# The first layer of both mixtures for the second half of the tokens by Strassen's 2x2 blocks (7 products for 8), with joined float32 weights kept in DRAM and read back

## Chip, cores and metric

The kernel runs on one core of one Trainium2 chip. The metric is device time in microseconds for one execution, here the median of the runs. In the texts "TensorE" is PE of the profile (PEld its weight loads), "VectorE" DVE, "ScalarE" ACT, "GpSimd" POOL, and SP is the queue that issues most DMAs.

## What is computed

An attention with two mixings of the heads (b = 4, 12 heads, 448 tokens of 64), then two layers on all 1792 tokens x 768:

```
h = (x @ w1) * (x @ w2) @ w3          # w1, w2: 768 x 1024, w3: 1024 x 1024
x = h @ w_out                         # w_out: 1024 x 768
h = maximum(x @ w_in, 0)              # w_in: 768 x 2048
return h * h @ w_out2                 # w_out2: 2048 x 768
```

All in float32; the kernel multiplies w3 by w_out once on the chip and uses the product.

## The kernel before

Attention takes the first third or so of the time; the change leaves it as it is. What follows is class `Moe`. The tokens lie in two halves `hf` of 896, each of two blocks `t` of 448 columns (`TB`). Feature chunks of 128 lie on the partitions.

A float32 product is made of three matmuls (`mm3`, L54): each operand is split into a high and a low part, w x = wh xh + wh xl + wl xh. A matmul has a 128x128 piece of weights and 448 columns of tokens.

The work of a half is a list of units. `l1` (16 units: eight output chunks `m`, for w1 and for w2) has 6 input chunks x 3 = 18 matmuls for each `t`; w1's result is copied to SBUF by ScalarE (L645), w2's is multiplied with it on VectorE (L649), and the product is split into `bhab` (ScalarE, L623) and `blab` (VectorE, L624). `ly` (6 units of 2 x 24 matmuls) multiplies by the joint w3 w_out. `l3` (16 units of 2 x 18, in two groups of 8) is the first layer of the second mixture: relu on ScalarE (L695), square on VectorE (L697), split into `bhh` and `blh`. `l4` (6 units of 2 x 24 after each group of l3) is its second layer.

Weights arrive as 64-bit words: `raw` by a DMA on SP (L69), `y` by a ScalarE copy (`narrow`, L81), three VectorE operations that put the float32 bits together (`join`, L93, L95, L97) into `f`. ScalarE then makes the high part `wh` (`high`, L111) and GpSimd the low part `wl` (`rest`, L115; VectorE for the pieces of w_out). There are 4 buffers of `raw`, 2 of `y`, 2 of `f`, 8 each of `wh` and `wl`. `stage(s)` sets the order on every engine: load piece s+6, narrow s+4, join s+3, low part of s+2, the unit's matmuls, high part of s+3. Each half brings all its weights through this chain anew; the first half also mixes the making of w3 w_out (`p34`) into l1.

## Time and profile before

| | |
|---|---|
| runs | 1362.34 us median (1362.15, 1362.34, 1362.64) |
| span of the profiled execution | 1361.7 us, that is 0.6 less than the median |
| its mean granted TensorE clock | 0.992 of full speed |
| first half: l1 with p34, ly, l3 and l4 | about 480 to 955 us |
| second half: l1 | 955 to 1070 us |
| second half: ly | 1070 to 1128 us |
| second half: l3, l4, l3, l4 | 1128 to 1362 us, some 57 us each |

The profile gives for each engine the time that it was busy. A stage's bound is read from the stage: which engine is busy without a break there, and what the others wait for. "Busy" counts an instruction from its start to its end, a stretch in which it waits for a port included.

### The profile page before, as it was taken

The page shows a single profiled execution, that of the slowest core. Times are in us where ns is not written, and L with a number is a line of the kernel's source. Part 1 is how long each engine was busy: PE and PEld are TensorE (multiplying, and loading weights), DVE is VectorE, ACT ScalarE, POOL GpSimd, SP SyncE. Part 2 cuts the span into 40 slices and gives each one's busy share as a digit, 9 for nine tenths or more (in the row PEclk, how much of TensorE's full clock was granted, in tenths as well). Part 3 has the DMA queues.
Part 4 walks back from the last instruction along what each step waited for, and adds up shares of the span by engine and source line. Part 5 has one row for each costly group of instructions (what it writes and reads, how often), then busy time and mean ns, then how long its engine had stood idle before and what let it go on. Part 6 is the DMA issues. An engine that isn't in the chain of part 4 may idle for free.

```text
span 1361.7 us, 23959 instructions
## 1 busy us (share of the span) xinstructions
PE 1318.2 (97%) x8858; PEld 1145.5 (84%) x8858; DVE 925.8 (68%) x1586; ACT 707.0 (52%) x1525; POOL 377.3 (28%) x399
## 2 busy tenths in 40 slices
PE   4999999999998799999999999999999999999998
PEld 2677777776776678899999999999999999999998
DVE  3798788788787689964218954985555228945972
ACT  4877878787886455534224533543343224533530
...
GB/s 145 189 176 189 123 198 198 138 168 203 144 122 170 119 164 168 189 181 131 60 66 109 128 119 79 121 185 181 120 117 95 62 78 101 133 120 80 124 149 57
DMA packets 97033, 183.76 MB, mean 135 GB/s; under 512 B 20693, under 2 KB 63701, under 8 KB 96469
## 3 DMA queue, kind: packets, MB, share of 16 engines
...
HBM read 129.52 MB, written 14.16 MB: 106 GB/s over the span
## 4 chain that ended last, share of the span: by engine, by line
PE 81%; issue 6%; ACT 4%; DVE 3%; POOL 3%; DMA 2%; SPq 0%; ACTq 0%; POOLq 0%; DVEq 0%
PE l L54 46%; PE y L54 8%; PE sp L281 7%; PE tp L337 5%; PE p L54 5%; PE pv L378 5%; PE sc L255 4%; ACT p L295 1%; POOL wl L115 1%; DMA r<-s 1%; POOL ql L238 1%; ACT ph L320 1%; ACT s L266 1%; DMA kraw<-k 1%; DVE pl L327 1%
## 5 line engine op out<-in xcount | busy, mean ns | idle before, releaser
L115 POOL TENSOR_TENSOR wl<-f,wh 128x384 fp32r<-128x384 f32 (+1 forms) x176 | 197.9, 1127 | 568.8 <-ACT wh L111 542.0
L93 DVE TENSOR_SCALAR f<-y 128x384 int32<-128x384 int32 (+1 forms) x208 | 149.3, 718 | 93.2 <-POOL wl L115 89.8
L281 PE MATMUL sp<-r,kpre 120*120 120x448 f32 x360 | 159.2, 564 | 6.2 <-DMA r<-s 3.5
L111 ACT ACTIVATE wh<-f 128x384 fp32r<-128x384 f32 (+1 forms) x192 | 106.7, 556 | 104.4 <-DVE f L97 96.1
L295 ACT ACTIVATE p<-sp,nm 120x448 f32<-120x448 f32 x180 | 113.7, 639 | 69.7 <-DVE nm L287 69.1
L54 PE MATMUL l<-bhh,wh 128*128 128x448 f32 x384 | 139.4, 363 | 0.0
L54 PE MATMUL l<-bhh,wl 128*128 128x448 f32 x384 | 139.2, 362 | 0.0
L54 PE MATMUL l<-blh,wh 128*128 128x448 f32 x384 | 138.2, 360 | 0.0
L287 DVE TENSOR_REDUCE nm<-sp 120x1 f32<-120x448 f32 x180 | 108.2, 620 | 41.5 <-PE sp L281 35.3
L97 DVE SCALAR_TENSOR_TENSOR f<-raw,f 128x384 int32<-128x384 int32 (+1 forms) x208 | 130.9, 629 | 7.2
L95 DVE SCALAR_TENSOR_TENSOR f<-y,f 128x384 int32<-128x384 int32 (+1 forms) x208 | 128.9, 620 | 7.0
L337 PEld LDWEIGHTS <-ph 120*128 120x128 f16 (+1 forms) x1440 | 108.0, 99 | 29.4 <-issue 28.9
L337 PE MATMUL tp<-kwh,ph 120*128 120x120 f16 x720 | 121.5, 219 | 3.8 <-DVE p L352 2.3
L327 DVE SCALAR_TENSOR_TENSOR pl<-p,sm,ph 120x448 f16<-120x448 f32 x180 | 124.5, 733 | 0.0
L337 PE MATMUL tp<-kwh,pl 120*128 120x120 f16 x720 | 120.7, 218 | 1.1 <-DVE pl L327 1.1
L81 ACT ACTIVATE y<-raw 128x384 f32<-128x384 f32 (+1 forms) x208 | 120.1, 577 | 1.5 <-DMA raw<-w3t 1.5
L337 PE MATMUL tp<-kwl,ph 120*128 120x120 f16 x720 | 120.7, 218 | 0.0
L320 ACT ACTIVATE ph<-p,sm 120x448 f16<-120x448 f32 x180 | 112.0, 683 | 16.0 <-DVE sm L315 15.8
L255 PE MATMUL sc<-kt,qh 128*110 128x448 f32 (+1 forms) x192 | 101.1, 527 | 16.2 <-DVE kt L216 14.6
L310 POOL TENSOR_SCALAR sm<-sm 120x2 f32<-120x2 f32 (+3 forms) x94 | 30.9, 329 | 273.0 <-ACT p L295 261.3
L281 PEld LDWEIGHTS sp<-r,kpre 120*120 120x120 f32 x360 | 58.9, 184 | 48.3 <-issue 21.4
L266 ACT ACTIVATE s<-sc 110x448 f32<-110x448 f32 (+1 forms) x186 | 90.5, 554 | 15.9 <-PE sc L255 15.9
(112 smaller groups left out, 3109.6 us busy)
## 6 DMA issues: line engine op xcount, KB each, us to landing
r<-s SPq DMA_DIRECT2D x172, 210.0 KB
...
```

The source lines that it names most:

```text
L54: nc.tensor.matmul(acc, w, x, start=(first and i == 0 and j == 0), stop=(last and i == n - 1 and j == 2))
L81: nc.scalar.activation(y, self.raw[i][:, :, 1].bitcast(F), AF.Copy, scale=2.0**-112)
L93: nc.vector.tensor_scalar(fi, yi, 3, 0x7FFFFFFF, ALU.logical_shift_left, ALU.bitwise_and)
L95: nc.vector.scalar_tensor_tensor(fi, yi, -0x80000000, fi, ALU.bitwise_and, ALU.bitwise_or)
L97: nc.vector.scalar_tensor_tensor(fi, raw[:, :, 0], 29, fi, ALU.logical_shift_right, ALU.bitwise_or)
L115: eng.tensor_tensor(self.out[i][1], self.ft.pop(i), f32(self.out[i][0]), ALU.subtract)
L255: nc.tensor.matmul(sc[:ic], t[:, hh * ic : hh * ic + ic], self.kt[b, h // 2][:, h % 2], start=(i == 0), stop=(i == 1))
L281: nc.tensor.matmul(t[:kk], self.kpre[:kk, :kk], self.rt.pop(g)[:kk], start=True, stop=True)
L295: nc.scalar.activation(p[:kk], self.sp.pop(g)[:kk], AF.Exp, bias=self.nm.pop(g)[:kk], accum_out=self.sm[g // 2][:kk, g % 2 : g % 2 + 1],)
L320: nc.scalar.activation(self.phl[g % NP][0][:kk, :S], self.pt[g][:kk], AF.Copy, scale=self.sm[g // 2][:kk, g % 2 : g % 2 + 1])
L327: nc.vector.scalar_tensor_tensor(l, self.pt.pop(g)[:kk], self.sm[g // 2][:kk, g % 2 : g % 2 + 1], h, ALU.mult, ALU.subtract)
L337: nc.tensor.matmul(t[:, j, :, :cnt], p[:kk, j * JP : j * JP + 128], w[:kk, :, :cnt], start=(i == 0), stop=(i == 2))
```

## The change

The first half runs as before, with one thing more: each piece of w1, w2, w_in and w_out2 that VectorE has joined is also stored to DRAM as float32 (`keep`, 88 stores on SP: 64 of 128x384, 24 of 128x512), and `f` has 4 buffers. The second half reads these back (`plain_weights` for ly and l4, `pair` for l1 and l3) and has no narrow and no join.

In the second half l1 and l3 are done in `pair`s. A pair has two `q`; each takes 2x2 blocks of weights (A11 to A22, 128x384 each) and 2x2 blocks of tokens and input chunks (B11 to B22), and makes four output blocks C from 7 products P1 to P7 of 9 matmuls instead of 8. The products come in the order P1, P2, P5, P6, P7, P4, P3, with q 0 and q 1 in turn. Three PSUM banks serve a q: A collects P1, P6, P7 and P4, B holds P2, C collects P5 and P3. ScalarE copies A to SBUF after P1, P6 and P7 (c1, c2, c3), and VectorE adds these copies and the banks. S1 to S4 are sums of weight blocks on GpSimd, T1 to T4 sums of token blocks, made once for x (`x_operands`, during the last l4 of the first half) and once for y (in ly). The highs of the weight operands are ScalarE's, the lows GpSimd's for P1, P5, P7 and P3, VectorE's for P2, P6 and P4. `gate` ends a pair of l1, `square` a pair of l3. There are four pairs of l1 and two for each of the two groups of l3.

The order on every engine in the second half comes from one list of events: each step has a time worked out from the pair's start `base` (1.8 a product, the highs 8 and the lows 6.5 ahead of the product, what follows a product 0.1 after it), and the steps are written out sorted by these times.

Also changed, with no part in the list above: the tokens' tiles of x and y are single tiles of 6 x 448 columns (tags `xy0` with 2 buffers and `xy1` with 5), the large tiles of results have 8 buffers in place of 10, the temporary tiles one tag with 7 buffers, and the pieces of w_out lie in other tiles.

```diff
+    wf = {
+        "w1": dram.tile([8, 128, DM], F, name="w1f"),
+        "w2": dram.tile([8, 128, DM], F, name="w2f"),
+        "win": dram.tile([16, 128, DM], F, name="winf"),
+        "wo2": dram.tile([6, 128, FF2], F, name="wo2f"),
+    }
...
-            self.w = Weights(wp, PW, 4, 2, 2, 8, 8)
+            self.w = Weights(wp, PW, 4, 2, 4, 8, 8)
...
+        def keep(self, i):
+            if i in self.w.ft and self.pieces[i].get("keep") is not None:
+                nc.sync.dma_start(self.pieces[i]["keep"], self.w.ft[i])
...
             if ok(s + 2):
-                w.rest(s + 2, nc.vector if self.pieces[s + 2][2:] else nc.gpsimd)
+                self.keep(s + 2)
+                w.rest(s + 2, nc.vector if self.pieces[s + 2].get("dve") else nc.gpsimd)
...
+            self.half1()
+            for _, _, f in sorted(self.events, key=lambda e: e[:2]):
+                f()
...
+        def plain_weights(self, tu, srcs):
+            w, keys = self.w, []
+            for i, src in enumerate(srcs):
+                k = ("p", round(tu, 3), i)
+                d = 2.4 * i
+                self.event(tu - 20 + d, lambda k=k, src=src: w.load(k, src, False))
+                self.event(tu - 12 + d, lambda k=k: (w.place(k), w.high(k)))
+                self.event(tu - 10 + d, lambda k=k: w.rest(k, nc.gpsimd))
+                keys.append(k)
+            return lambda: [w.out[k] for k in keys]
...
+        def pair(self, base, srcs, ops, finish):
+            DUR, w, T = 1.8, self.w, {}
+            order = ("P1", "P2", "P5", "P6", "P7", "P4", "P3")
+            need = {
+                "P1": ("A11", "B11", "A"), "P2": ("A12", "B21", "B"), "P5": ("S1", "T1", "C"),
+                "P6": ("S2", "T2", "A"), "P7": ("S3", "T3", "A"), "P4": ("A22", "T4", "A"), "P3": ("S4", "B22", "C"),
+            }
+            opened = {"P1", "P2", "P5"}
+            for q in range(2):
+                def load(j, q=q):
+                    t = self.w.p.tile([128, 2 * HC], F, tag="raw", name=f"q{base}_{q}_{j}", bufs=4)
+                    nc.sync.dma_start(t, srcs[q][j])
+                    T[q, f"A{j + 1}1"], T[q, f"A{j + 1}2"] = t[:, :HC], t[:, HC:]
+                def add(n, a, b, op, q=q):
+                    t = self.w.p.tile(
+                        [128, PW], F, tag="y" if n == "S4" else "f", name=f"{n}_{base}_{q}", bufs=2 if n == "S4" else 4
+                    )
+                    T[q, n] = t[:, :HC]
+                    nc.gpsimd.tensor_tensor(T[q, n], T[q, a], T[q, b], op)
+                b = base + 1.8 * q
+                self.event(b - 16, lambda load=load: load(0))
+                self.event(b - 12, lambda load=load: load(1))
+                for at, a in (
+                    (-4.0, ("S1", "A21", "A22", ALU.add)), (-2.8, ("S2", "S1", "A11", ALU.subtract)),
+                    (-1.6 + 5.0 * q, ("S3", "A11", "A21", ALU.subtract)), (-0.4 + 5.0 * q, ("S4", "A12", "S2", ALU.subtract)),
+                ):
+                    self.event(b + at + 2.0 * q, lambda a=a, add=add: add(*a))
+            for i, pn in enumerate(order):
+                for q in range(2):
+                    t0 = base + DUR * (2 * i + q)
+                    an, bn, bank = need[pn]
+                    def hi(q=q, an=an, pn=pn):
+                        T[q, pn, "w"] = tuple(
+                            w.p.tile([128, PW], R, tag=f"w{e}", name=f"w{e}{base}_{q}{pn}", bufs=8)[:, :HC] for e in "hl"
+                        )
+                        nc.scalar.activation(T[q, pn, "w"][0], T[q, an], AF.Copy)
+                    def lo(q=q, an=an, pn=pn, eng=(nc.gpsimd if i % 2 == 0 else nc.vector)):
+                        h, l = T[q, pn, "w"]
+                        eng.tensor_tensor(l, T[q, an], f32(h), ALU.subtract)
+                    def go(q=q, pn=pn, bn=bn, bank=bank):
+                        if pn in opened:
+                            T[q, bank] = self.psum(f"{bank}{base}_{q}")
+                        h, l = T[q, pn, "w"]
+                        x = ops()[bn]
+                        mm3(
+                            T[q, bank],
+                            [
+                                ((h[:, 128 * c : 128 * c + 128], l[:, 128 * c : 128 * c + 128]), (x[0][:, c], x[1][:, c]))
+                                for c in range(3)
+                            ],
+                            pn in opened, True, pn not in opened,
+                        )
+                    self.event(t0 - 8, hi)
+                    self.event(t0 - 6.5, lo)
+                    self.event(t0, go)
+                    end = t0 + DUR
+                    def after(q=q, pn=pn):
+                        cp, tt = nc.scalar.activation, nc.vector.tensor_tensor
+                        A, B_, C = (T.get((q, x)) for x in "ABC")
+                        if pn == "P1":
+                            T[q, "c1"] = self.tmp(f"c1{base}_{q}")
+                            cp(T[q, "c1"], A, AF.Copy)
+                        elif pn == "P2":
+                            tt(T[q, "c1"], B_, T[q, "c1"], ALU.add)
+                            finish(q, "C11", T[q, "c1"], None)
+                        elif pn == "P6":
+                            T[q, "c2"] = self.tmp(f"c2{base}_{q}")
+                            cp(T[q, "c2"], A, AF.Copy)
+                        elif pn == "P7":
+                            T[q, "c3"] = self.tmp(f"c3{base}_{q}")
+                            cp(T[q, "c3"], A, AF.Copy)
+                            tt(T[q, "c3"], C, T[q, "c3"], ALU.add)
+                            finish(q, "C22", T[q, "c3"], None)
+                        elif pn == "P4":
+                            finish(q, "C21", None, A)
+                        elif pn == "P3":
+                            tt(T[q, "c2"], C, T[q, "c2"], ALU.add)
+                            finish(q, "C12", T[q, "c2"], None)
+                    self.event(end + 0.1, after)
...
+        def gate(self, base, m):
+            keep = {}
+            def finish(q, block, z, bank):
+                ab = ("ab1", m + q)
+                if block == "C11":
+                    self.xy[ab] = self.big(f"ab1_{m + q}")
+                    keep[q, "a0"] = z
+                elif block == "C22":
+                    keep[q, "b1"] = z
+                elif block == "C21":
+                    z = keep[q, "a0"]
+                    nc.vector.tensor_tensor(z, bank, z, ALU.mult)
+                    self.split(self.xy[ab], slice(0, TB), z)
+                else:
+                    nc.gpsimd.tensor_tensor(z, z, keep[q, "b1"], ALU.mult)
+                    self.split(self.xy[ab], slice(TB, HT), z)
+            return finish
+        def square(self, base, f):
+            def finish(q, block, z, bank):
+                i = f + 2 * q + (block[1] == "2")
+                ts = slice(0, TB) if block[2] == "1" else slice(TB, HT)
+                if ("h1", i) not in self.xy:
+                    self.xy["h1", i] = self.big(f"h1_{i}")
+                if bank is not None:
+                    z = self.tmp(f"r1_{i}")
+                    nc.scalar.activation(z, bank, AF.Relu)
+                    nc.gpsimd.tensor_tensor(z, z, z, ALU.mult)
+                else:
+                    nc.vector.scalar_tensor_tensor(z, z, 0.0, z, ALU.max, ALU.mult)
+                self.split(self.xy["h1", i], ts, z)
+            return finish
...
+        def half1(self):
+            T = 0.0
+            ops = self.x_operands(-44.0)
+            for m in range(0, 8, 2):
+                self.pair(T, [(wf["w1"][m + q], wf["w2"][m + q]) for q in range(2)], ops, self.gate(T, m))
+                T += 14 * 1.8
+            D = {}
...
+            for gr in range(2):
+                for f in range(0, 8, 4):
+                    i = 8 * gr + f
+                    self.pair(
+                        T, [(wf["win"][i + 2 * q], wf["win"][i + 2 * q + 1]) for q in range(2)],
+                        lambda: D["y"], self.square(T, i),
+                    )
+                    T += 14 * 1.8
```

How the order of ScalarE stands in the second half's l3, first before: one high part, one narrowing copy, one relu and one high part of a result for each unit and `t` (`wh178` is piece 178, `r1_0_0` half 1, unit 0, t 0).

```order
L111 ACTIVATE wh178_12926<-f178_12922 128x384
L81 ACTIVATE y180_12959<-raw180_12879 128x384
L695 ACTIVATE r1_0_0_12989<-l3_1_0_0_12970 128x448
L111 ACTIVATE wh179_12965<-f179_12961 128x384
L81 ACTIVATE y181_12996<-raw181_12918 128x384
L623 ACTIVATE bhh1_0_12968<-h21_0_0_12991 128x448
L695 ACTIVATE r1_0_1_13026<-l3_1_0_1_13007 128x448
L111 ACTIVATE wh180_13002<-f180_12998 128x384
```

After, at the end of the first pair of the first group of l3 and the beginning of the second. 158.4 is the base of the first pair and 183.6 of the second; the digit behind it is q, P1 and so on the product whose weight high is made (L872); L911 is the copy c3, L951 the relu of C21, L637 the high part of a result.

```order
L872 ACTIVATE 183.60000000000005_0P1_13151<-183.60000000000005_0_0_13078 128x384
L911 ACTIVATE c3158.40000000000006_1_13163<-A158.40000000000006_1_12992 128x448
L637 ACTIVATE bhh1_3_13166<-c3158.40000000000006_1_13163 128x448
L872 ACTIVATE 183.60000000000005_1P1_13172<-183.60000000000005_1_0_13093 128x384
L951 ACTIVATE r1_1_13184<-A158.40000000000006_0_12963 128x448
L637 ACTIVATE bhh1_1_13145<-r1_1_13184 128x448
L872 ACTIVATE 183.60000000000005_0P2_13190<-183.60000000000005_0_0_13078 128x384
L951 ACTIVATE r1_3_13204<-A158.40000000000006_1_12992 128x448
L637 ACTIVATE bhh1_3_13166<-r1_3_13204 128x448
L872 ACTIVATE 183.60000000000005_1P2_13212<-183.60000000000005_1_0_13093 128x384
L637 ACTIVATE bhh1_0_13035<-c2158.40000000000006_0_13108 128x448
```

The highs of the second pair's weights now stand in ScalarE's queue behind result highs and relus of the first pair, one and one.

GpSimd in the same place, before (low parts of pieces 177 to 181, and nothing else there):

```order
L115 TENSOR_TENSOR wl177_12888<-f177_12883,wh177_12887 128x384
L115 TENSOR_TENSOR wl178_12927<-f178_12922,wh178_12926 128x384
L115 TENSOR_TENSOR wl179_12966<-f179_12961,wh179_12965 128x384
L115 TENSOR_TENSOR wl180_13003<-f180_12998,wh180_13002 128x384
L115 TENSOR_TENSOR wl181_13040<-f181_13035,wh181_13039 128x384
```

And after (L876 low parts of weights, L952 the square of C21, L853 the sums S1 to S4, the number ahead of the base saying which):

```order
L876 TENSOR_TENSOR 183.60000000000005_0P1_13152<-183.60000000000005_0_0_13078,183.60000000000005_0P1_13151 128x384
L952 TENSOR_TENSOR r1_1_13184<-r1_1_13184 128x448
L876 TENSOR_TENSOR 183.60000000000005_1P1_13173<-183.60000000000005_1_0_13093,183.60000000000005_1P1_13172 128x384
L853 TENSOR_TENSOR 1_183.60000000000005_0_13193<-183.60000000000005_0_1_13110 128x384
L952 TENSOR_TENSOR r1_3_13204<-r1_3_13204 128x448
L853 TENSOR_TENSOR 2_183.60000000000005_0_13210<-1_183.60000000000005_0_13193,183.60000000000005_0_0_13078 128x384
L853 TENSOR_TENSOR 3_183.60000000000005_0_13228<-183.60000000000005_0_0_13078,183.60000000000005_0_1_13110 128x384
L853 TENSOR_TENSOR 4_183.60000000000005_0_13234<-183.60000000000005_0_0_13078,2_183.60000000000005_0_13210 128x384
L853 TENSOR_TENSOR 1_183.60000000000005_1_13236<-183.60000000000005_1_1_13127 128x384
L876 TENSOR_TENSOR 183.60000000000005_0P5_13232<-1_183.60000000000005_0_13193,183.60000000000005_0P5_13231 128x384
L853 TENSOR_TENSOR 2_183.60000000000005_1_13253<-1_183.60000000000005_1_13236,183.60000000000005_1_0_13093 128x384
```

Between the low parts of the second pair's weights now stand squares of the first pair and the weight sums.

SP in the first half, in the stage with p34, before:

```order
L69 DMA raw16_7205<-wo 128x768
L69 DMA raw17_7215<-w2 128x768
L69 DMA raw18_7250<-w2 128x768
L69 DMA raw19_7262<-wo 128x768
L69 DMA raw20_7293<-w1 128x768
L69 DMA raw21_7328<-w1 128x768
L69 DMA raw22_7361<-wo 128x768
```

And after, where L499 is the store of a joined piece (`w1f` and `w2f` are the copies in DRAM):

```order
L75 DMA raw16_7206<-wo 128x768
L75 DMA raw17_7216<-w2 128x768
L75 DMA raw18_7251<-w2 128x768
L499 DMA w1f_59<-f14_7220 128x384
L75 DMA raw19_7264<-wo 128x768
L499 DMA w1f_59<-f15_7255 128x384
L75 DMA raw20_7295<-w1 128x768
L75 DMA raw21_7330<-w1 128x768
L499 DMA w2f_60<-f17_7299 128x384
L75 DMA raw22_7364<-wo 128x768
```

Each store of a piece of w1 or w2 is put behind the load of the piece that is four further on.

## Rows read from the trace of the kernel before

**Rows 1.** The page, part 1: busy us (share of the span) and instructions by engine.
```profile
PE 1318.2 (97%) x8858; PEld 1145.5 (84%) x8858; DVE 925.8 (68%) x1586; ACT 707.0 (52%) x1525; POOL 377.3 (28%) x399
```

**Rows 2.** Chain that ended last, in time: start us, us, engine, tile, line, count.
```profile
724.48 345.60 PE l L54 x1728
1070.08 57.60 PE y L54 x288
1127.68 230.42 PE l L54 x1152
```

**Rows 3.** Windows: us, busy PE, PEld, DVE, ACT, POOL; PEclk, DMA share, GB/s.
```profile
480.00:500.00 20.00, 17.89 (x87) 16.20 (x88) 15.55 (x29) 10.48 (x21) 2.65 (x2) 1.00 0.55 172
500.00:520.00 20.00, 19.18 (x92) 16.70 (x91) 19.31 (x34) 10.57 (x22) 5.44 (x5) 1.00 0.60 168
520.00:540.00 20.00, 18.71 (x90) 16.22 (x90) 19.41 (x35) 9.73 (x21) 5.47 (x5) 1.00 0.58 159
540.00:560.00 20.00, 20.00 (x100) 18.47 (x99) 18.31 (x34) 10.67 (x24) 5.47 (x5) 1.00 0.58 169
...
955.00:1070.00 115.00, 115.00 (x577) 107.79 (x576) 58.90 (x118) 43.50 (x90) 33.15 (x32) 1.00 0.37 106
...
1128.00:1185.00 57.00, 57.00 (x287) 53.43 (x286) 52.98 (x77) 30.03 (x63) 17.36 (x16) 1.00 0.41 123
```

**Rows 4.** Tiles x1h and y1h: ns min/median/max, first and last start, shape.
```profile
L54 PE MATMUL l<-x1h,wh x192: 363/363/363, 954.7 to 1069.3; 128*128 128x448 f32 x192
...
L54 PE MATMUL l<-y1h,wh x192: 363/363/363, 1127.5 to 1299.7; 128*128 128x448 f32 x192
```

**Rows 5.** Lines by form, 955 to 1350 us: busy us, mean ns, idle before.
```profile
L115 POOL TENSOR_TENSOR wl<-f,wh 128x384 fp32r<-128x384 f32 x61 | 62.7, 1032 | 166.4 <-ACT wh L111 158.8 <-PE y L54 3.8 <-PE l L54 3.8
...
L97 DVE SCALAR_TENSOR_TENSOR f<-raw,f 128x384 int32<-128x384 int32 x61 | 34.0, 558 | 2.1
...
L111 ACT ACTIVATE wh<-f 128x384 fp32r<-128x384 f32 x61 | 31.6, 518 | 6.5 <-DVE f L97 6.5
...
L697 DVE TENSOR_TENSOR h<-r 128x448 f32<-128x448 f32 x32 | 20.0, 624 | 9.9 <-ACT r L695 9.9
...
L624 DVE TENSOR_TENSOR blh<-h,bhh 128x448 fp32r<-128x448 f32 x32 | 19.8, 618 | 0.0
...
L695 ACT ACTIVATE r<-l 128x448 f32<-128x448 f32 x32 | 17.5, 546 | 54.5 <-PE l L54 54.5
...
L115 POOL TENSOR_TENSOR wl<-raw,wh 128x512 fp32r<-128x512 f32 x12 | 15.6, 1307 | 38.9 <-ACT wh L111 38.9
```

**Rows 6.** The page, part 5, the narrowing copy: busy us, mean ns, idle before.
```profile
L81 ACT ACTIVATE y<-raw 128x384 f32<-128x384 f32 (+1 forms) x208 | 120.1, 577 | 1.5 <-DMA raw<-w3t 1.5
```

**Rows 7.** Timeline at two places of l3/l4: start us, us, engine, line, operation.
```profile
1183.16 1.43 POOL L115 TENSOR_TENSOR wl<-f,wh 128x512 fp32r<-128x512 f32 x1 [2.54 <-ACT wh L111]
1183.35 1.53 DVE L93 TENSOR_SCALAR f<-y 128x512 int32<-128x512 int32 x1
...
1190.74 0.42 DVE L93 TENSOR_SCALAR f<-y 128x512 int32<-128x512 int32 x1
...
1191.20 0.69 DVE L95 SCALAR_TENSOR_TENSOR f<-y,f 128x512 int32<-128x512 int32 x1
1191.26 1.78 POOL L115 TENSOR_TENSOR wl<-f,wh 128x512 fp32r<-128x512 f32 x1 [2.71 <-ACT wh L111]
...
1191.92 1.67 DVE L97 SCALAR_TENSOR_TENSOR f<-raw,f 128x512 int32<-128x512 int32 x1
```

**Rows 8.** Timeline of GpSimd and of VectorE at 487 us, and VectorE's L613, x0l.
```profile
486.82 1.64 POOL L613 TENSOR_TENSOR x0l<-x0l,x0h 128x660 fp32r<-128x660 f32 x1 [5.63 <-ACT x0h L611]
...
487.42 2.55 DVE L613 TENSOR_TENSOR x0l<-x0l,x0h 128x660 fp32r<-128x660 f32 x2 [0.45 <-ACT x0h L611]
...
L613 DVE TENSOR_TENSOR x0l<-x0l,x0h x3: 848/884/1739, 486.1 to 489.1; 128x660 fp32r<-128x660 f32 x2, 128x708 fp32r<-128x708 f32 x1
```

**Rows 9.** Source line L649 (one input in PSUM), 560 to 1362 us.
```profile
L649 DVE TENSOR_TENSOR p<-l,a x22: 616/625/625, 563.6 to 1070.1; 128x448 f32<-128x448 f32 x22
```

369 lines of the change are left out of this document (243 added, 126 removed).

## The prediction

> **What bounds the kernel now.** I read the page's busy shares first, then the chain of waits in order of time, then busy time by stage. The shares say TensorE: it is busy for 97% of the span, VectorE for 68%, ScalarE for 52%, GpSimd for 28% [rows 1]. The chain says where this is strict: its last links are TensorE alone, 1728 matmuls in 345.60 us, 288 in 57.60, 1152 in 230.42 [rows 2], which is 0.200 us a matmul each time, so from 724 us to the end TensorE never waits and the time is a count of matmuls. Much earlier it is not strict: from 480 to 540 us TensorE is busy for 17.89, 19.18 and 18.71 of 20 us while VectorE shows 15.55, 19.31 and 19.41 [rows 3]; there the joins of the weights set the pace. The changed stages of the second half lie in the strict part: its l1 runs from 954.7 to about 1070, and its l3 in two groups between 1127.5 and 1300 [rows 4]. In those stages the other engines have room: in 115 us of l1 VectorE is busy for 58.90, ScalarE for 43.50, GpSimd for 33.15; in the first group of l3 (57 us) for 52.98, 30.03 and 17.36 [rows 3].
>
> **What the change removes.** l1 and l3 of the second half are 32 units of 2 x 18 = 36 matmuls, 1152. As eight pairs of 2 x 7 products of 9 matmuls they are 1008. The 144 that go are worth 144 x 0.200 = 28.8 us, if TensorE stays fed. The profiled span is 1361.7 us, so that alone makes 1332.9; the median of the runs is 0.6 above the span, so 1333.5. The joins and narrowings of the second half's weights go too (three VectorE operations and one ScalarE copy for each of 88 pieces; one of the three takes 34.0 us for the 61 pieces of 128x384 in the window of the rows [rows 5]). They sit beside TensorE work and nothing waits for them there, so they are worth nothing by themselves; they only make room.
>
> **What it adds in the first half.** 88 stores of joined pieces (64 of 192 KB, 24 of 256 KB) on SP. Each stands behind the load of the same stage and waits for a join that is one stage older than the one for which the next load waits, so nothing queued behind it is held longer. The DMA engines are 0.55 to 0.60 busy in 480 to 560 us at 159 to 172 GB/s [rows 3]; 16 stores of 192 KB in those 80 us add about 40 GB/s, which makes the share roughly 0.7, an estimate. VectorE's joins stay the bound there. Price: from -2 (four buffers for joined pieces in place of two, so the join waits less for GpSimd) to +4 us (one late load each 20 us); I take 0: in the whole run the narrowing copy on ScalarE waits 1.5 us in all for a raw piece [rows 6].
>
> **What it adds in the second half.** A pair takes 126 x 0.200 = 25.2 us of TensorE. In that time GpSimd must make 8 weight sums and 8 low parts of 128x384. The same operation on the same shape takes 1.032 us [rows 5]: 16.5 us. Two operations of 128x448 come on top (the square of C21 in l3, the product of C12 in l1); between 1.032 for 384 columns and 1.307 for 512 [rows 5] that is about 1.17 each, so 18.8 us. VectorE in a pair of l3 ("square") makes 6 low parts of weights (about 0.56, as L97's two-input operation on that shape, 0.558), 6 squares (about 0.62, as L697's 0.624) and 8 low parts of results (0.618) [rows 5]: 3.4 + 3.7 + 4.9 = 12.0 us with both inputs in SBUF, and 6 additions of a PSUM bank (0.62 each, 3.7 us). ScalarE has 14 highs (0.518), 6 copies and 2 relus (0.546) and 8 result highs (about 0.55 too) [rows 5]: 16.0 us. Each alone fits in 25.2.
>
> **VectorE and GpSimd together do not.** The rows show that the two don't run side by side for such operations. At 1183.35 a VectorE TENSOR_SCALAR, 0.42 long at 1190.74, starts 0.19 after GpSimd's and lasts 1.53, to just behind GpSimd's end; at 1191.92 the two-input operation, 0.69 at 1191.20, lasts 1.67, to 0.55 after GpSimd's end. The other way round GpSimd's, begun at 1191.26 under the running VectorE operation, lasts 1.78 [rows 7] where 1.307 is usual [rows 5]. A tensor_tensor of two SBUF inputs does the same: of three, one lasts 1.739 against 0.848 for the shortest, the one that starts at 487.42 under GpSimd's of 486.82 [rows 8]. With one input in PSUM nothing is stretched: L649 is 616 to 625 ns in all 22, many beside GpSimd [rows 9]. So of a square pair 18.8 + 12.0 = 30.8 us have to go one after the other in 25.2. The last row of that group has 0.14 us of the waiting operation's 0.69 hidden at the hand-over; with 20 turns each way that hides at most 5.6, which brings 30.8 down to 25.2. So a pair has from 0 to 5.6 us too much, the four square pairs 0 to 22.4. In a pair of l1 ("gate") VectorE has only 6 weight lows and 4 result lows with two SBUF inputs, 3.4 + 2.5 = 5.9, so 18.8 + 5.9 = 24.7: it fits, barely. In the first l3 group of before, GpSimd's 17.36 and VectorE's 52.98 us add to more than the 57 [rows 3], as waiting for the port counts as busy, and TensorE lost nothing: a piece's low there is made two stages, 7.2 us, ahead of its unit, and each engine had little else that TensorE waits for.
>
> The Trainium skill has this as a rule: in "SBUF — State Buffer", section "Who interferes with whom", the port that VectorE and GpSimd share is locked for the whole instruction by whoever starts first, for a VectorE instruction of two SBUF inputs against a GpSimd one that reads SBUF. The rows agree on who waits, and differ in the 0.14 us that they hide. By the rule as it stands, nothing is hidden, the four square pairs are the whole 22.4 us late, and the time is 1333.5 + 22.4 = 1355.9, where the rows allow anything from 1333.5 up to that.
>
> **Which wait ends last.** So I followed the queues of the second square pair of a group with these durations, from the first pair's first matmul (the order pieces show ACT and POOL there). P7 of q 0 ends at 16.4; its copy c3, VectorE's addition and square are done at 18.35, and ScalarE stands at the high of C22 until then. Behind that wait stand the next pair's first high and the copy c3 of q 1, done at 20.1, which P4 of q 1 needs at 19.8: 0.3 late. Then relu of C21 at 23.0, GpSimd's square to 24.2, ScalarE standing at its high until 24.8; the same for q 1, where GpSimd's square comes behind two weight operations, at 27.75; ScalarE's high 28.35. VectorE's low of it and then the next pair's P2 low at 30.6, wanted at 29.55: 1.1 late. The P2 low of q 1 comes behind the addition, square and low of C12: 34.9 for 32.45, 2.4 late. Then the low of P6 for q 1, 1.8, and the copy c2, which stands in ScalarE's queue behind two highs of results and four of weights, 2.8. Together 8.4 us a group; without the shared port it comes to 4 (0.3 + 1.2 + 2.4). Bounds for both groups: 0 (all slack where I see none) to 22.4. I take 2 x 8.4, about 17, because the trace's stretched rows are exactly of these operations. Gate pairs: the low of P5 for q 1 on GpSimd is done at 9.0 to 9.35 of the pair and wanted at 9.4; I take 0, bounds 0 to 5.9 a pair. The way into l1, from ly into the first square pair, and the sums of x and y have slack of 0.25 to 0.5 us each by the same count; 0, bound +2. The unchanged stages (l4, ly) keep their matmuls, and their lows, on GpSimd as before for w34d, now face no joins.
>
> **Sum**: 1361.7 - 28.8 + 17 = 1349.9 as a span, 1350.5 beside the runs; I say 1350.
>
> **Rivals.** (1) The queues don't bite: the shared port hides its part at each hand-over, or the fixed orders have more slack than I count. Then the stalls are 0 to 11 us, the 8 of both groups without the port as its middle: 1333.5 + 8 = 1341.5. For it: every engine alone has a third of its time free; against: [rows 7, 8]. (2) The stalls reach the gate pairs in part: 1 to 3 us each, 4 to 12 in all on top of 17, so 1355 to 1362, say 1358. For it: 24.7 of 25.2 leaves no room for any waiting in order; against: no result chain of two engines lies ahead of weights there, save C12's product. (3) Slower than before: in the gate pairs each of the ten two-input VectorE operations takes the port just ahead of a GpSimd operation on TensorE's path, so that the whole 5.9 is seen in each, 4 x 5.9 = 23.6 on top of 17: 1333.5 + 40.6 = 1374. It decides from 28.8 - 17 = 11.8 in four pairs, 2.95 us a pair. Against it: in l1 of the half before, two-input operations beside GpSimd delayed nobody. (4) The change doesn't do what it says: the saved matmuls are gone by count (by the order the new TensorE queue is the old one with 144 fewer matmuls, all of them in l1 and l3 of the second half), so I give it nothing.
>
> **How the numbers follow.** Forecast, stalls of 11 to 22 us (1344.5 to 1355.5): 0.47. Rival 1: 0.25. Rival 2: 0.16, a little of which lies within 0.2% of before. Rival 3: 0.12. A measurement of this kernel can tell 0.2%, 2.7 us, from no change; faster by more means below 1359.6: 0.47 + 0.25 + 0.09 = 0.81; within 0.2%, 0.07; slower, 0.12. The range takes in the forecast, rival 2, and rival 1 down to stalls of 3 us, and with them the +4 of the stores only where it lies inside: 1337 to 1362. It leaves out 0.12 above and some 0.07 below. Most of the chance is on one sign.
>
> **What would show it.** TensorE at 0.200 us a matmul with 1008 matmuls in the first layers; idle TensorE of about 17 us, nearly all between the second pair's P2 and P6 of each l3 group, released by VectorE's lows and ScalarE's c2; l1 of the second half about 101 us with at most 2 us idle; two-input VectorE operations of about 1.2 us beside GpSimd; 480 to 560 us as before within 2 us. Wrong if TensorE is idle in the gate pairs too, if idle time is released by DMA (the read-back), or if the stretch before 560 us grows.

## The result and the profile after

| | before | after |
|---|---|---|
| median | 1362.44 us (1362.15 to 1362.64, 4 runs) | 1370.16 us (1369.97 to 1370.59, 4 runs) |
| profiled span | 1361.7 us | 1368.5 us |

The ratio of the runs is 1.0057, 95% interval 1.0043 to 1.0072: slower by about 8 us, where 12 us less were forecast. TensorE's busy time hardly fell although 144 matmuls are gone; the page's part 1 of the changed kernel, to hold against [rows 1]:

```profile
PE 1313.6 (96%) x8714; PEld 1119.8 (82%) x8714; DVE 875.3 (64%) x1428; ACT 700.2 (51%) x1518; POOL 495.3 (36%) x499
```

144 matmuls fewer (8714 for 8858), and only 4.6 us less of busy time. The chain of waits of the changed kernel, in order of time (start us, us, engine, tile, line, count), shows the first and largest loss. It answers to [rows 2]:

```profile
666.72 59.14 PE y L60 x288
...
1072.58 59.14 PE y L60 x288
...
1188.51 59.14 PE l L60 x288
...
1305.71 59.15 PE l L60 x288
```

The 288 matmuls of `ly`, which the change doesn't touch, took 57.60 us before and take 59.14 now, in both halves, and so do those of `l4`. That is 205.3 ns a matmul for 200.0. No wait stands between them; each starts later after the one ahead. The timeline of TensorE in the second half's `ly` shows it (start us, us, engine, line, operation), the changed kernel first:

```profile
1091.72 0.36 PE L60 MATMUL y<-blab,wh('p', 110.4, 1)_12534 128*128 128x448 f32 x1
1091.93 0.37 PE L60 MATMUL y<-bhab,wl('p', 110.4, 1)_12535 128*128 128x448 f32 x1
...
1092.75 0.36 PE L60 MATMUL y<-bhab,wh('p', 120.0, 0)_12578 128*128 128x448 f32 x1
1092.95 0.37 PE L60 MATMUL y<-blab,wh('p', 120.0, 0)_12578 128*128 128x448 f32 x1
```

and the same stage of the kernel before:

```profile
1091.72 0.36 PE L54 MATMUL y<-blab,wh 128*128 128x448 f32 x1
1091.92 0.36 PE L54 MATMUL y<-bhab,wl 128*128 128x448 f32 x1
...
1092.72 0.36 PE L54 MATMUL y<-bhab,wh 128*128 128x448 f32 x1
1092.92 0.36 PE L54 MATMUL y<-blab,wh 128*128 128x448 f32 x1
```

From 1091.72, six matmuls later stands 1092.95 where 1092.92 stood: five thousandths of a microsecond each, some 4000 times. A step this small is lost in the rounding of single rows; the chain's row over 288 of them shows it.

The windows of the changed kernel that answer to [rows 3] (us, busy PE, PEld, DVE, ACT, POOL; PEclk, DMA share, GB/s):

```profile
480.00:500.00 20.00, 18.52 (x90) 16.46 (x89) 15.85 (x31) 10.70 (x21) 1.64 (x1) 1.00 0.59 185
500.00:520.00 20.00, 19.57 (x94) 17.19 (x94) 19.48 (x33) 9.87 (x21) 6.46 (x6) 1.00 0.79 207
520.00:540.00 20.00, 18.74 (x89) 15.97 (x88) 18.73 (x36) 11.02 (x24) 4.69 (x5) 1.00 0.77 210
...
955.00:1070.00 115.00, 112.41 (x542) 100.89 (x541) 65.96 (x80) 50.40 (x105) 88.92 (x78) 1.00 0.25 83
1128.00:1185.00 57.00, 54.29 (x255) 48.40 (x254) 36.10 (x48) 26.50 (x58) 41.89 (x37) 0.97 0.19 56
```

The stores are there (DMA share 0.77 to 0.79 for 0.58 to 0.60, somewhat over the forecast's 0.7) and cost the mixed stage nothing. VectorE has lost the joins in l3 (36.10 us for 52.98), GpSimd has more (41.89 for 17.36), and TensorE is no longer busy throughout: 54.29 of 57. What TensorE waited for after 890 us (engine, line, waited for: us in total, times, longest us; the name of a bank begins with the last digits of its pair's base, so 3.6 is the second pair of the first l3 group, 1.6 of the second):

```profile
PE l L60 <- POOL wl L121: 4.8, 3, 2.2
PE 1.60000000000014_0_14166 L60 <- ACT 1.60000000000014_0_14302 L908: 1.9, 1, 1.9
PE 3.60000000000005_1_13292 L60 <- DVE .60000000000005_1P L876: 1.9, 1, 1.9
PE 1.60000000000014_1_14220 L60 <- DVE .60000000000014_1P L876: 1.9, 1, 1.9
PE 3.60000000000005_0_13238 L60 <- ACT 3.60000000000005_0_13374 L908: 0.8, 1, 0.8
```

The last four are in the second pair of each l3 group, released by VectorE's low of P2 for q 1 and by ScalarE's copy c2. The first is not in l3: the last l4 of the first half waits for GpSimd's weight lows.

So the loss has two parts: a slower pace everywhere, and waits in three places. Measured stage by stage from the starts of the matmuls, where the duration of a pair counts from its first matmul to the next stage's first:

| kernel | ns per matmul in ly | last l4 of the first half | l1 pairs | pairs of l3, first and second group | span |
|---|---|---|---|---|---|
| before | 200.0 | 57.6 | (28.8 for the same) | (28.8 for the same) | 1361.7 |
| after | 205.3 | 64.7 | 26.6, 26.2, 26.2, 26.2 | 25.8, 31.0; 25.8, 32.2 | 1368.5 |
| e1 | 200.0 | 65.7 | 25.3 each | 25.5, 30.9; 25.4, 32.3 | 1353.7 |
| e5 | 202.2 | 64.8 | 25.5 each | 25.5, 32.2; 25.5, 32.2 | 1359.8 |
| e6 | 202.2 | 64.7 | 25.5 each | 25.5, 32.1; 25.5, 32.1 | 1360.4 |
| e7 | 202.2 | 63.6 | 26.5, then 25.5 each | 25.5, 26.7; 25.5, 26.7 | 1352.3 |
| e8 | 202.2 | 62.3 | 27.7, then 25.5 each | 25.5, 32.2; 25.5, 32.2 | 1358.0 |
| e9 | 200.0 | 65.2 | 25.2 each | 25.4, 32.2; 25.3, 31.0 | 1350.3 |
| e10 | 200.0 | 66.0 | 25.2 each | 25.2, 26.6; 25.2, 26.6 | 1339.8 |
| e11 | 200.0 | 63.4 | 25.2 each | 25.2, 26.6; 25.2, 26.6 | 1338.3 |
| e12 | 200.0 | 60.8 | 26.4, then 25.2 each | 25.2, 26.6; 25.2, 26.6 | 1336.2 |

(The attention and the first unit behind it end at 477 to 482 us in these profiles, without a part in the argument; that is why spans are compared to some 3 us only, and stages to 0.1.)

### The profile page after: what moved, and what is told of

Same layout as the page of the kernel before. It is cut to its first block, busy times and chain, and to the rows that moved or that the text cites. A ratio compares the mean times of both kernels' runs of the same rounds, so it can differ in the third digit from the quotient of the medians.

```text
span 1368.5 us, 23487 instructions
## 1 busy us (share of the span) xinstructions
PE 1313.6 (96%) x8714; PEld 1119.8 (82%) x8714; DVE 875.3 (64%) x1428; ACT 700.2 (51%) x1518; POOL 495.3 (36%) x499
## 4 chain that ended last, share of the span: by engine, by line
PE 68%; issue 8%; DVE 7%; ACT 6%; POOL 6%; DMA 4%; SPq 1%; ACTq 0%; POOLq 0%; DVEq 0%
PE l L60 27%; PE y L60 9%; PE sp L287 6%; PE p L60 5%; PE tp L343 5%; PE sc L261 4%; PE pv L384 4%; ACT p L301 2%; DMA kraw<-k 1%; ACT ph L326 1%; ACT s L272 1%; POOL wl L121 1%; DMA xb<-xd 1%; POOL ql L244 1%; DVE f L99 1%
## 5 line engine op out<-in xcount | busy, mean ns | idle before, releaser
L121 POOL TENSOR_TENSOR wl<-f,wh 128x384 fp32r<-128x384 f32 (+1 forms) x88 | 102.5, 1166 | 310.0 <-ACT wh L117 297.5
L343 PEld LDWEIGHTS <-ph 120*128 120x128 f16 (+1 forms) x1440 | 107.8, 99 | 29.2 <-issue 28.8
L99 DVE TENSOR_SCALAR f<-y 128x384 int32<-128x384 int32 (+1 forms) x120 | 93.8, 782 | 40.9 <-ACT y L87 40.8
L358 DVE TENSOR_SCALAR p<-tp,iv 112x480 f32<-112x480 f32 (+1 forms) x135 | 90.9, 701 | 3.0 <-PE tp L343 2.7
L117 ACT ACTIVATE wh<-f 128x384 fp32r<-128x384 f32 (+1 forms) x104 | 58.4, 562 | 66.5 <-DVE f L103 58.3
L384 PE MATMUL pv<-p,v 112*64 112x110 f32 (+1 forms) x1536 | 83.0, 266 | 1.8 <-DVE p L358 1.2
L101 DVE SCALAR_TENSOR_TENSOR f<-y,f 128x384 int32<-128x384 int32 (+1 forms) x120 | 80.1, 668 | 4.0
L384 PEld LDWEIGHTS pv<-p,v 112*64 112x64 f32 x1536 | 76.0, 140 | 5.3 <-ACT y L87 1.4
L103 DVE SCALAR_TENSOR_TENSOR f<-raw,f 128x384 int32<-128x384 int32 (+1 forms) x120 | 75.9, 632 | 4.1
L261 PE MATMUL sc<-kt,ql 128*110 128x448 f32 (+1 forms) x192 | 75.0, 391 | 2.1 <-POOL ql L244 1.2
```

The costliest lines, as they stand in the source:

```text
L99: nc.vector.tensor_scalar(fi, yi, 3, 0x7FFFFFFF, ALU.logical_shift_left, ALU.bitwise_and)
L121: eng.tensor_tensor(self.out[i][1], self.ft.pop(i), f32(self.out[i][0]), ALU.subtract)
L261: nc.tensor.matmul(sc[:ic], t[:, hh * ic : hh * ic + ic], self.kt[b, h // 2][:, h % 2], start=(i == 0), stop=(i == 1))
L343: nc.tensor.matmul(t[:, j, :, :cnt], p[:kk, j * JP : j * JP + 128], w[:kk, :, :cnt], start=(i == 0), stop=(i == 2))
L384: nc.tensor.matmul(t[64 * e : 64 * e + 64, x, :ic], self.v[b][:, j, g], self.p2[n][:, j, g, :ic], start=(j == 0), stop=(j == JC - 1),)
```

## The experiments

### Where the operands lie: e1, e2, e3

The kernel before keeps 24 unused elements ahead of its first token tile and 48 behind its second (`new_xy`, `before, after = 24, 0` and `0, 48`). The change makes both plain tiles. In the built programs this moves the weights' tiles: they begin at 160 modulo 256 bytes of a partition before, at 128 now, and the tokens of block t = 0 at 224 and 128. Theory A: the place sets the pace. Rival B: something else that the change brings does (stores, read-back, GpSimd's work).

e1 moves the operands of the changed kernel by an unused 32 bytes:

```diff
             self.wp = wp
+            wp.tile([128, 8], F, tag="pad", name="pad", bufs=1)
```

> The changed kernel with one unused tile of 32 bytes a partition ahead of everything in the pool that holds the weights and the first token tiles. In it, as in the kernel before, every operand of the float32r matmuls begins at 32 modulo 64 bytes; in the changed kernel all weights begin at 0 modulo 64, and part of the tokens. Theory A (the place of the operands sets the pace): a matmul of 448 columns starts every 200.0 ns instead of 203.5 to 205.4, which by the counts of the trace after gives back 20.2 us; with pairs of 25.2 instead of 25.9 us there is less slack in l3, whose stalls may grow from 11.9 towards the 17 of the prediction: 1350 to 1355. Theory B (the pace comes from something else that the change brings, such as the stores, the read-back or GpSimd's added work beside TensorE): the pace stays at 205.3 and the time at 1370 +- 1.

Measured: 1356.86 us beside 1364.16 of before in the same runs, ratio 0.9949 (0.9933 to 0.9966). The chain:

```profile
664.86 57.60 PE y L60 x288
...
1063.14 57.60 PE y L60 x288
```

The old pace is back in these stages, and with it a gain over the kernel before. A holds, though not quite as expected: the 787 matmuls that read the first token tiles took 202.9 ns and not 200.0, and the time lies 1.9 us above the 1350 to 1355 (the kernel before took 1364.16 us in the same runs for 1362.44 above). The l3 stalls came to 12.8 us, nearer to the 11.9 than to the 17: second pairs of 30.9 and 32.3 us, 5.7 and 7.1 above 25.2.

e2 takes the unused elements from the kernel before and changes nothing else:

```diff
-            for e, before, after in (("h", 24, 0), ("l", 0, 48)):
+            for e, before, after in (("h", 0, 0), ("l", 0, 0)):
```

> The kernel before without the unused 24 and 48 elements that it keeps beside its first two token tiles; nothing else differs. Weights then begin at 0 modulo 64, the tokens of block t = 0 of l1 and l3 at 0, all others at 32, as in the changed kernel. Theory A: 3264 matmuls 5.4 ns (3.3 for the 384 of 384 columns) and 1152 matmuls 3.6 ns slower: 15.6 + 1.3 + 4.1 = 21 us, so 1383 +- 2. Theory B: 1362 +- 1.

Measured: 1383.19 us beside 1364.16, ratio 1.0139 (1.0115 to 1.0163). The chain:

```profile
669.83 59.14 PE y L54 x288
728.97 353.71 PE l L54 x1728
1082.68 59.14 PE y L54 x288
```

59.14 us, the changed kernel's number to the last digit, in a kernel with no Strassen, no stores and no read-back. B falls.

e3 puts the 32 bytes between the first token tiles and the weights:

```diff
-            return tuple(self.six(t, f"{name}{e}{t}") for e in "hl")
+            out = tuple(self.six(t, f"{name}{e}{t}") for e in "hl")
+            if t == 0 and name == "x":
+                self.wp.tile([128, 8], F, tag="pad", name="pad", bufs=1)
+            return out
```

> The changed kernel with the unused 32 bytes between the first token tiles and the weights: all weights begin at 32 modulo 64, 816 matmuls read tokens at 0 modulo 64, the other 3456 at 32. It tells weights from tokens. If the weights' place alone counts, all matmuls of 448 columns start every 200.0 ns, as in e1. If the tokens' place counts too, the 816 are slower than 200.0 by some ns, and the time is up to 3 us above e1.

Measured: 1357.17 us in one run, span 1355.4 beside 1353.7 of e1. The 787 matmuls with the tokens at 128 start every 204.4 ns, the rest every 200.1. The tokens' place counts as well as the weights'.

### Is it modulo 64, 128 or 256: e5, e9

e5 was to restore the places of before modulo 128, as a base for the experiments on the stalls (unused tiles of 96 bytes ahead of the first token tiles and 64 behind, 512 bytes of DMA scratch in place of 1024 to make room).

```diff
+            wp.tile([128, 24], F, tag="pad", name="pad", bufs=1)
...
+                self.wp.tile([128, 16], F, tag="pad2", name="pad2", bufs=1)
...
-    nc = bacc.Bacc("TRN2", target_bir_lowering=False, num_devices=1, dynamic_dma_scratch_size=1024)
+    nc = bacc.Bacc("TRN2", target_bir_lowering=False, num_devices=1, dynamic_dma_scratch_size=512)
```

> The changed kernel with unused tiles of 96 bytes ahead of the first token tiles and 64 bytes behind them (and 512 bytes less of DMA scratch to make room), which puts every operand where the kernel before had it modulo 128 bytes too: weights at 32, tokens at 96. In e1 the units that read the first token tiles (at 32 modulo 128 there) took 203 ns a matmul. If those bytes are why, the l1 pairs go from 25.33 to 25.2 us and each l3 of the first half from 58.03 to 57.6, some 2 us in all; if not, they stay. The second pair of each l3 group stays at 31 to 32 us and the last l4 of the first half at 65 to 66. Span 1351 to 1353.

Measured: 1361.54 us in one run, span 1359.8: a miss. Every matmul of 448 columns took 202.2 ns, in units of first and other token tiles alike.

```profile
666.27 58.24 PE y L60 x288
...
1065.95 58.24 PE y L60 x288
```

Modulo 128 all operands stood as before; modulo 256 the weights stood at 32 and not at 160. e9 puts that right by 48 elements behind the token tiles, just what the kernel before had:

```diff
-                self.wp.tile([128, 16], F, tag="pad2", name="pad2", bufs=1)
+                self.wp.tile([128, 48], F, tag="pad2", name="pad2", bufs=1)
```

> The changed kernel with unused tiles of 96 bytes ahead of the first token tiles and 192 bytes behind them (and 512 bytes less of DMA scratch): the operands of the float32r matmuls then stand as in the kernel before modulo 256 bytes, weights at 160 and tokens at 224. In e5, where they stood alike only modulo 128 (weights at 32), every matmul of 448 columns took 202.2 ns. If modulo 256 is what counts: 200.0 in all stages, l1 pairs 25.2 us, each l3 of the first half 57.6; second square pairs 31 to 32, last l4 of the first half 65 to 66; span 1351 to 1353. If something else set 202.2, it stays 202.2 and the span near 1360. This is the change itself, at the operand places of the kernel before.

Measured: 1351.67 us beside 1361.69, ratio 0.9924 (0.9907 to 0.9941), span 1350.3 for the 1351 to 1353 expected.

```profile
663.50 57.60 PE y L60 x288
721.10 182.41 PE l L60 x912
1059.93 57.60 PE y L60 x288
```

200.0 in all stages. e9 is the change itself at the operand places of the kernel before: 10 us faster where the change as it is was 8 us slower. The paces by place, from all starts of consecutive matmuls less than 230 ns apart (places from the built programs):

| weights begin at, modulo 256 | tokens at | in | matmuls of 448 columns | ns from start to start |
|---|---|---|---|---|
| 160 | 224 | before, e9 | 4004, 3817 | 200.0, 200.05 |
| 32 | 224 | e5 | 3810 | 202.2 |
| 160 | 160 | e1 | 787 | 202.9 |
| 128 | 128 | after, e2 | 787, 1130 | 203.5, 203.4 |
| 160 | 128 | e3 | 787 | 204.4 |
| 128 | 224 | after, e2 | 3026, 2877 | 205.35, 205.3 |

The mean pace goes with the pair of places; neither operand's place alone gives it, and modulo 64 or 128 doesn't either. It is not the whole of it. In e1 the pair 160/160 gives 202.4 ns in the first half's l3 and 205.3 in its l1 at 540 to 565 us, and 160/224 gives 200.3 over all of e1 and 200.1 in e3. For 384 columns it is 173.35 and 176.65 ns at 160/224 and 128/224, but at 32/224 174.7 in e5 and e6 and 176.7 in e7 and e8, where these operands stand at the same addresses to the byte. What else counts there, why one place is better than another, and whether more than 256 bytes count, was not tried.

### Why the second square pair stalls: e6, e7

The prediction held the port that VectorE and GpSimd share and the standing queues responsible together. e6 takes two-input work away: sums of banks are written back to PSUM, squares and products become VectorE operations with one PSUM input, and C21's square and C12's product leave GpSimd.

```diff
-                            tt(T[q, "c1"], B_, T[q, "c1"], ALU.add)
-                            finish(q, "C11", T[q, "c1"], None)
+                            finish(q, "C11", T[q, "c1"], B_)
...
+                if block == "C22":
+                    nc.vector.scalar_tensor_tensor(z, z, 0.0, z, ALU.max, ALU.mult)
+                else:
+                    if block == "C21":
+                        z = self.tmp(f"r1_{i}")
+                        nc.scalar.activation(z, bank, AF.Relu)
+                    else:
+                        nc.vector.tensor_tensor(bank, bank, z, ALU.add)
+                        nc.vector.tensor_scalar(z, bank, 0.0, None, ALU.max)
+                    nc.vector.tensor_tensor(bank, bank, z, ALU.mult)
+                    z = bank
+                self.split(self.xy["h1", i], ts, z)
```

> e5, and results are finished in their PSUM banks: sums of banks are written back to the bank, the squares of C11, C12 and C21 and the products of l1 are VectorE operations with one PSUM and one SBUF input, C21's square and C12's product leave GpSimd, and the low part is taken from the bank. Two-input SBUF work of VectorE and GpSimd in a square pair falls from 30.8 to 22.4 us; the order of ScalarE stays. Theory of the port alone: the second pairs fall from 31-32 to 25.2-26 us. Prediction's theory (port and standing queues): 28 to 29 us. Order of the queues alone: 30 us or more. Span between 1339 and 1352 accordingly; the l4 of 65 us stays.

e7 moves no work between engines; it issues each result's split 2.0 us after the product's end:

```diff
-                self.split(self.xy["h1", i], ts, z)
+                self.later(end + 2.0, self.xy["h1", i], ts, z)
...
+        def later(self, t, dst, ts, p):
+            self.event(t, lambda: self.split(dst, ts, p))
```

> e5, and the split of each result (ScalarE's high, VectorE's low) is issued 2.0 us after the product's end by the event list instead of 0.1, so that ScalarE doesn't stand waiting for the square ahead of the next weights' highs. No work is added or removed. Order of the queues alone: the second pairs fall from 31-32 to 25.2-26.5 us. Port alone: 30 us or more, since 30.8 us of two-input work stay. Both: 27 to 30.

Measured: e6 1362.44 us (span 1360.4, above the 1339 to 1352 expected), e7 1354.11 us, beside 1361.54 of e5, one run each. The windows of the second pair of the first l3 group (columns as above), e5, e6 and e7 in this order:

```profile
1149.39:1181.61 32.22, 28.11 (x128) 24.64 (x127) 19.68 (x27) 14.71 (x31) 21.15 (x19) 0.95 0.18 49
```

```profile
1150.18:1182.31 32.13, 28.13 (x127) 24.62 (x126) 22.64 (x35) 14.76 (x31) 16.10 (x16) 0.95 0.19 50
```

```profile
1153.37:1180.03 26.66, 25.75 (x128) 23.54 (x127) 23.94 (x28) 15.04 (x31) 23.27 (x19) 1.00 0.23 60
```

GpSimd is 5 us less busy in e6 and the pair is as long as before; GpSimd and VectorE are both at 23 to 24 us of 26.66 in e7 and the pair is 5.6 us shorter (0.16 over what the order alone was expected to give). The port alone falls: in e7 all the two-input work stays, VectorE's weight lows beside GpSimd are even longer (1.36 us in the median of all, 1.08 in e5), and all but 1.2 us of the stall goes. A change of the order is enough for that. What share the port has under the old order is not shown. The 28 to 29 us of the prediction's mixture did not come in e6, but e6 is not clean, since C11 and C12 have one VectorE operation more in it and VectorE is 3 us busier: the wait for P2's low fell (1.9 to 0.7 us in the waits of the pair), as the mixture would have it, while those for c2 and for P6's low grew (1.9 to 2.4, 0.3 to 0.9).

The granted clock shows a second price: 0.95 over the stalled pairs, 1.00 in e7. In the changed kernel the matmuls behind the 1.86 us wait start every 0.373 us for some 3 us, at half the clock (1.2 GHz for 2.4); the timeline (idle before in brackets; the last row is nine matmuls in 3.47 us, where nine start within 1.85 at the full clock):

```profile
1161.07 2.14 PE L60 MATMUL 3.60000000000005_0_13274<-ys,.60000000000005_0P 128*128 128x448 f32 x9
...
1165.48 1.82 PE L60 MATMUL 3.60000000000005_1_13292<-ys,.60000000000005_1P 128*128 128x448 f32 x7 [1.86 <-DVE .60000000000005_1P L876]
1167.10 3.47 PE L60 MATMUL 3.60000000000005_0_13314<-ys,.60000000000005_0P 128*128 128x448 f32 x9
```

Not every such wait has this price. The second pairs of e9, first and second group, have the same waits by the profile:

```profile
PE 1.60000000000014_0_14168 L60 <- ACT 1.60000000000014_0_14304 L912: 1.9, 1, 1.9
PE 3.60000000000005_0_13240 L60 <- ACT 3.60000000000005_0_13376 L912: 1.9, 1, 1.9
PE 3.60000000000005_1_13294 L60 <- DVE .60000000000005_1P L880: 1.9, 1, 1.9
PE 1.60000000000014_1_14222 L60 <- DVE .60000000000014_1P L880: 1.9, 1, 1.9
```

and yet the clock fell in the first alone (windows, columns as above), which is 1.24 us longer:

```profile
1142.80:1175.03 32.23, 27.94 (x128) 24.55 (x126) 20.11 (x26) 13.79 (x30) 20.70 (x19) 0.95 0.18 49
1257.91:1288.90 30.99, 26.59 (x127) 23.24 (x126) 19.99 (x26) 13.67 (x29) 20.77 (x19) 1.00 0.18 51
```

The order that makes the waits can be read in the changed kernel. ScalarE's timeline there (L637 a result's high, L872 a weight's):

```profile
1158.73 0.58 ACT L637 ACTIVATE bhh<-r 128x448 fp32r<-128x448 f32 x1 [1.81 <-POOL r L952]
1159.22 0.51 ACT L872 ACTIVATE .60000000000005_1P<-60000000000005_1_0_13093 128x384 fp32r<-128x384 f32 x1
1162.83 0.58 ACT L637 ACTIVATE bhh<-8.40000000000006_0_13108 128x448 fp32r<-128x448 f32 x1 [3.11 <-DVE 8.40000000000006_0_13108 L954]
```

and VectorE's (L638 a result's low, L876 a weight's low, L917 a sum):

```profile
1159.35 0.81 DVE L638 TENSOR_TENSOR blh<-r,bhh 128x448 fp32r<-128x448 f32 x1 [2.41 <-ACT bhh L637]
1160.08 1.36 DVE L876 TENSOR_TENSOR .60000000000005_0P<-60000000000005_0_0_13078,.60000000000005_0P 128x384 fp32r<-128x384 f32 x1
...
1163.45 0.71 DVE L638 TENSOR_TENSOR blh<-8.40000000000006_0_13108,bhh 128x448 fp32r<-128x448 f32 x1 [0.65 <-ACT bhh L637]
1164.08 1.34 DVE L876 TENSOR_TENSOR .60000000000005_1P<-60000000000005_1_0_13093,.60000000000005_1P 128x384 fp32r<-128x384 f32 x1
```

Each engine stands for the other's step of the first pair's results (1.81, 2.41, 3.11, 0.65 us) with the second pair's weights behind it; the low of P2 for q 1, whose high was ready at 1159.73, ends at 1165.42, and TensorE starts at 1165.48. The lows of 1.36 and 1.34 us, where the six that run beside no GpSimd instruction take 0.55, are the shared port: some 0.8 us each, a part of this delay; how much of the 1.86 us would be left without it, no clean run shows.

The Trainium skill's rule on that port ("SBUF — State Buffer", section "Who interferes with whom": a VectorE instruction of two SBUF inputs and a GpSimd one that reads SBUF exclude each other for the whole instruction) describes these two rows. The 22.4 us in four square pairs that the prediction worked out by it came in no run: e7 has the same two-input work and loses 1.2 us in each of two pairs.

### The last l4 of the first half: e8, e11, e12

The sums and splits of the second half's tokens lie in this l4. e8 takes two-input work away there, on the base of e5:

```diff
-                    D["T1"] = self.tmp(f"x1{c}")
+                    D["T1"] = self.psum(f"x1{c}")
...
-                    ("T1", nc.gpsimd), ("T3", nc.vector), ("T2", nc.gpsimd), ("T4", nc.vector),
-                    ("B11", nc.gpsimd), ("B21", nc.vector), ("B22", nc.gpsimd),
+                    ("T1", nc.vector), ("T3", nc.vector), ("T2", nc.vector), ("T4", nc.vector),
+                    ("B11", nc.gpsimd), ("B21", nc.gpsimd), ("B22", nc.gpsimd),
```

> e5, and the sums T1 to T4 of the tokens x are written to PSUM by VectorE, their low parts all taken by VectorE from PSUM, the lows of B11, B21, B22 by GpSimd. In the last l4 of the first half two-input SBUF work falls from about 64 us (VectorE 12 joins of 1.8, 12 sums of 0.62, 9 lows of 0.62; GpSimd 24 operations of 1.2 to 1.3) to about 51, in 57.6 us of TensorE. Theory of the port: that l4 falls from 65.7 to 58-60 us. Rival (GpSimd's weight lows come late because of their place in the order, behind token highs of ScalarE): 63 or more. Everything else as e5.

Measured: 1359.75 us in one run. The l4 fell from 64.8 to 62.3 us, between the two expectations, and the first l1 pair rose from 25.5 to 27.7: 0.2 us less in all.

The changed kernel's VectorE shows another cause, the first sum waiting for its load:

```profile
920.94 0.63 DVE L795 TENSOR_TENSOR x<-xb,xs 128x448 f32<-128x448 f32 x1 [2.76 <-DMA xb<-xd]
```

SP issues that load at 915.12, 5.8 us ahead of the sum, behind three others (`xs<-xd`, 913.71) and beside the loads and stores of l4's weights. First e10, which is e9 with the late split of e7:

> e9, and the split of each result issued 2.0 us after the product's end as in e7. From e7 (second pairs 26.66 us at 202.2 ns a matmul, 1.2 above the first pairs) second pairs of 26.4 to 27 us at 200.0 ns; against e9 some 10 us less: 1341 to 1344 beside 1362.3 of before.

Measured: 1342.63 us beside 1361.69, ratio 0.9856 (0.984 to 0.9873). Second pairs of 26.6 us, as expected; the l4 stays at 66.0. Then e11, e10 with the loads earlier:

```diff
-                self.event(s - 7.0, lambda c=c: load(c))
+                self.event(s - 13.0, lambda c=c: load(c))
```

> e10, and the loads of the second half's tokens for the sums T are put 13 instead of 7 us ahead of the first sum. In the traces so far VectorE stands at the first sum for 2 to 3 us waiting for that load, with the joins of the next weight pieces behind it. If that starts the lateness of the last l4 of the first half, its 64 to 66 us fall by 3 to 6, and the time to 1336 to 1340. If the sums and lows themselves are too much for VectorE and GpSimd there, it stays above 62.5 and the time within 2 us of e10.

Measured: 1340.08 us, ratio 0.9841 (0.9825 to 0.9857). The wait at the first sum is gone:

```profile
909.02 0.62 DVE L805 TENSOR_TENSOR x<-xb,xs 128x448 f32<-128x448 f32 x1
```

The l4 falls by 2.6 us to 63.4, less than the 3 to 6 expected; the late load was a part only. Of the 2.6, 1.0 is waiting (3.4 us of TensorE's waits for GpSimd's weight lows in this l4 for 4.4); the rest goes with the clock, which falls to half for some 3 us twice in e10's l4 (behind the starts at 926.7 and 950.3), once in e11's and not in e12's, in the one profile of each. The medians of e10 and e11 differ by 2.6 us, within the scatter of their four runs each (1340.8 to 1343.6, 1338.9 to 1343.4), so the gain is read from the stage. e12 adds e8's edit to e11:

> e11, with the token sums T1 to T4 of x in PSUM and their lows all on VectorE, as in e8. In e11 the last l4 of the first half still takes 63.4 us for 57.6, in three waits for lows of its weights on GpSimd. If two-input work of VectorE and GpSimd sets that, it falls to 58 to 60 us and the time to 1335 to 1337. If the lateness is one of order (GpSimd standing for ScalarE's highs of the tokens, which stand for VectorE's sums), or only moves into the first l1 pair as in e8 (27.7 us there), the time stays within 2 us of e11, 1338 to 1342 beside 1361.7.

Measured: 1339.59 us beside 1361.85, ratio 0.9835 (0.9814 to 0.9856). The l4 falls to 60.8, the first l1 pair rises to 26.4: l4 and pair together are 1.5 us shorter, the time is that of e11 within the interval. What is left there (3.2 us of waits by the profile, all of TensorE for GpSimd's lows: 2.6 in l4, 0.6 in the pair) stays open between too much two-input work and its order. e11 and e12 are the best versions: 1.6% faster than the kernel before.

## Why the prediction was wrong, point by point

**The step that failed is the first one**: "which is 0.200 us a matmul each time, so from 724 us to the end TensorE never waits and the time is a count of matmuls". The count was right, the price of one was taken as fixed. It changes with where the operands lie, and the edit that moved them (two padded token tiles made plain ones) was not costed at all. By the table of paces it took 3026 x 5.35 + 787 x 3.5 + 371 x 3.3 ns = 20.2 us. The trace of before could not give this number, since all operands of class `Moe` stood at one pair of places. It had a sign, though: the attention's score matmuls (L255) have 448 float32r columns too, with weights at other places in steps of 8 bytes, and started in the mean 198.2 ns apart with weights at 120 modulo 256 (4 matmuls) and 207.0 with weights at 96 (7 matmuls). The unused 24 and 48 elements, in a diff line that removed them, were another, that the place may have been chosen. The third rival, "slower than before", was given with another mechanism (the port in the gate pairs), and that one didn't happen: e9's l1 pairs are 25.2 us.

**The saving** of 28.8 us was right at the old pace: in e9 the l1 pairs and the first l3 pairs take 25.2 to 25.4 us for 28.8.

**The stalls of l3** were forecast at 8.4 us a group, in the second pair, at P2 and c2. They are there, at these products: 5.1 and 6.4 us in the changed kernel (30.98 and 32.23 for 25.84, the first pairs' length), 7.2 and 5.9 in e9. The term of 17 us was too large by 5 in the changed kernel and by 4 in e9, and a part of what was measured is the half clock behind a wait, which the forecast did not have: at the full clock a group takes 5.9 us (e9's second), 4.2 of it in the waits of the profile, where 8.4 were forecast. Of its cause the chain of standing queues was right (e7 removes all but 1.2 us of 6.7 by order alone); the shared port is not needed for it and does not make it alone (e7), and its share stays open (e6).

**The gate pairs** were taken at nothing; the changed kernel has 1.6 us in the four (26.6 + 3 x 26.2 for 4 x 25.87 at its pace), e9 none.

**The way into l1** was taken at nothing, with a bound of 2 us. It cost 5.6 us in the changed kernel (64.73 for 59.14) and 7.6 in e9, where the waits are 5.2 and the clock fell once. The step missed the loads of the sums (a queue and a landing time that the prediction did not follow) and what the sums and token lows put ahead of l4's joins and weight lows on VectorE and GpSimd.

**The stores** were taken at nothing, with -2 to +4. In e9, at the old pace, the rest of the mixed l1 takes 85.6 us for 86.4 and the first unit of p34 11.7 for 12.7: about -1.8, near the lower bound.

Put together for e9: 1361.7 - 28.8 + 13.1 (l3) + 7.6 (l4) - 1.8 (mixed stage) - 1.6 (attention and the first unit behind it end at 479.0 for 480.6) = 1350.2, and its span is 1350.3. The changed kernel is this with 20.2 us of slower pace, in which the stalls of l3 and l4 come out 3.6 us smaller, and the gate pairs' 1.6. Of the 2.0 us less in l4, 0.4 is waiting (4.8 for 5.2 us); the clock fell there in e9 and not in the changed kernel. In l3 the wait for c2 in the first group is 0.8 us for 1.9. That the longer products leave the other engines more time would explain it and is not shown.

So the forecast of 1350 would have stood for the change at the old places, and there partly by luck, since errors cancel: l3 taken 3.7 too long, the mixed stage 1.8, the attention 1.6, l4 7.6 too short.
